# Transposing four normalised attention rows on TensorE instead of by DMA, with a new step list, in a gated SSM and linear-attention kernel

## The chip, the core and the metric

The kernel runs on one core of a Trainium2 chip. The time is device microseconds of one execution; lower is better. The profile is of one further execution. Engines: PE is TensorE (PEld its weight loads), DVE VectorE, ACT ScalarE, POOL GpSimd, SP the engine that issues most DMAs.

## The reference

The input x has 2048 rows of 512 (bf16). Two branches are computed from it and mixed, row by row, with a gate:

```python
g = sigmoid((x * gate_w).sum(-1, keepdims=True))
a = 2.0 * einsum("blp,dp->bld", h, C).real + x * Dskip   # h[t] = Lam_bar * h[t-1] + B_bar x[t], 512 complex states
q, k, v = split(x @ wqkv)                                # 32 heads of 16
phi(u) = concat(softmax(u @ w_phi), softmax(-(u @ w_phi)))
b = ((phi(q) @ (phi(k).T @ v)) / (phi(q) . sum(phi(k)) + 1e-6)) @ wo
out = g * a + (1 - g) * b
```

## The kernel before

The 2048 rows are taken as 16 tiles of 128; the rows of one tile share their index modulo 8 (`r`), so that the recurrence becomes eight interleaved ones of 256 steps. All tiles and weights stay in SBUF.

The program is written as small generators, one for each piece of work, and each `yield` ends a step. The string ORDER, a list of some 850 names, says in which order the steps are emitted; each engine then runs its own instructions strictly in that order, and waits on semaphores where data or a PSUM bank is not ready. In a name, `@5` gives the PSUM bank of the step, `:D` puts a copy out of PSUM on DVE instead of ACT, `:A` issues an output DMA from ACT instead of SP, and `F:36` emits 36 constant 128-column products on PE (L802) that keep PE busy and are not used.

The steps that matter here:

- `l8` to `l15`: SP loads one tile of x by a transposing DMA (L228); tiles 0 to 7 are loaded at the head of the program. `NR`, `NI`: SP loads the two halves of B into Bn (L283). `R0` to `R7`: SP transposes Bn into BT (L287). `Q`, `C`: SP transposes the query weights and C (L291, L295). `J`: SP moves C's parts into X1 and X2 (L300). `O`: SP loads Wo (L304).
- `W`, `f`: PE transposes the key weights C2r (L273) and folds w_phi into them (L430). `k`, `v`, `q`: PE projects a tile to keys, values or queries (L474, four 512-column matmuls), and ACT or DVE copies the bank out. `g<r><j>`: PE computes the inputs of the recurrence (L600 to L607, reading BT), and ACT copies to uv. `z`: the scan on DVE. `h<r><j>`: the states. `c`: two products by ACT from X1, X2 (L589) and a sum by DVE give the output matrix.
- `x`, `n`, `e`, `s` (and `X`, `N`, `E`, `S` for queries, in groups of four rows): maximum, minimum, exponential and normalisation of the features. The last steps of `S1` to `S3` issue four transposing DMAs each from SP, phT<-EEq (L562), the feature maps of four rows.
- `a`, `Y`: the sum over keys and its masked copy KVm.
- For each of the 16 output tiles n: `y` collects the SSM output in a PSUM bank (L716, two steps of four 512-column matmuls, then L721, four of 128); `o` has two halves of four 68-column matmuls pn (L735), from which ACT takes the logarithm of the denominator (ld) and ACT or DVE a copy (nu), then rd on ACT and the normalised row `on` on DVE (L743), then the transpose oT<-on by a DMA from SP (L748); `t` adds oT times Wo into the same bank (L755, four of 512), scales (L759, L761) and issues the output DMA (L763).

Two of these pieces, as they stand:

```python
oT = op_.tile([P, HG, P], BF16, name="oT", bufs=8)
live["oT", n] = oT
nc.sync.dma_start_transpose(out=oT[:], in_=on[:].rearrange("p g h e -> p (g h e)"))
```

Of the kernel before, what the change touches and what calls it, by code (L numbers as in the profile page):

```python
# [23 lines left out]
ORDER = """
NR B F:36 F:6 W0@0 W0:D NI W1@1 W2@2 W3@3 W1 f0@4 f0 W2:D W3:D f1@5 f2@6 f2:D f1 f3@0 f3 F:6 l9 V@1 V U U P k0@2 P P
V2@3 k0 P2 P2 U P2 V2 k1@4 k1 l10 P2 P2 P4 U P4 P3 P2 P3 k3@5 k2@7 P4 i0 i3 i0 i0 k2 i0 i3 v3@6 n0 v1@0 v0@1 x0 n0
k5@3 i3 i3:D i2 i0 l11 k6@2 l14 i3 x0 gw n0 i2 x0 k4@4 i1 v1 v6@7 k3 i2 i2:D x0 i1 l8 x0 i2 i1 i1:D i1 x1 n0 x1 n0 M
x1 n1 x1 n1 x1 n1 k5:D n1 L R0 k7@0 k7:D k6 k4 v3 n1 x2 R1 e0 e0 n2 l12 s0 n2 v5@5 v2@2 v2 e1 s0 n2 s0 v7@4 n2 v4@3 v4
k9@6 e1 k10@0 l15 x2 k11@2 s0 R5 l13 x2 s1 k8@3 x2 Q3 k10 s1 s0 s0 s0 v5 v6 v7 v0 k14@0 s1 g40@5 k14 D Q0 g00@7 g00 R3
s1 k8 a0@41 k12@0 a0 g40 x2 k12 n2 s1 s1 s1 k9 g20@7 g10@3 R2 g10 g20 Q1 g10 k11 x3 g50@5 n3 x3 n3 x3 n3 g30@0 g60@6  # L30
C0 e2 e2 x3 g60 a1 e2 a1 e2 k13@7 C5 g30 g30 n3 k15@3 k15 k13 x3 g21@2 n3 s2 s2 e3 C4 e3 x4 R4 s2 g01@6 g01 g50 g21
g50 x4 s2 g11@0 g41@3 s2 g51@7 s2 n4 g11 g70@6 x4 n4 g31@2 x4 n4 g11 s2 e3 e3 s3 Q2 g70 g70 g61@5 g70 z0 g41 z0 s3
w2@0 g31 g31 C6 n4 a2 C1 s3 g61 C2 C3 a2 a2 z0 C7 w3@6 a2 w3 g51 x4 g51 w2 n4 w0@3 w0 g02@2 z0 w1@5 w1 s3 g71@6 z0 g02
J2 g71 g71 g12@7 z0 g71 v8@0 J3 e4 e4 z1 v8 J2 g22@3 s3 g12 g22 z0 z0 g62@5 z1 z0 z0 q1@2 z1 s3 z1 z1 z1 R6 q0@6 J1
g12 J0 s3 q2@0 J3 e4 q0 z1 z1 e4 s4 g32@3 z1 z1 q3@7 q2 q1 q3 c2 s4 g32 g42@6 g42 xA g52@0 h10@2 h50@7 h50 R7 g43@6 J1
g62 g32 g52 c5 c5 J0 g52 g43 g03@5 nA xA c4 h60@3 c4 g72@7 h10 g72 g72 g72 h51@0 h11@6 v9@2 v9 h60 v11@3 c5 c1 xA nA
c1 h51 z2 s4 z2 g03 s4 v11 g23@0 g23 h61@7 z2 a3 O v10@2 v10 z2 z2 g63@5 g63 g13@3 g13 nA h11 nA a3 a3 c4 z2 a3 c0 g13
c1 z2 z2 xA z2 z2 h61 xA g33@6 g33 h12@0 c3 c3 c0 c0 s4 s4 g33 v14@2 v14 h12 g53@5 g53 g53 nA s4 h52@3 h52 eA g73@7
g73 h20@0 g73 g73 z3 z3 eA eA eA v12@6 v12 v15@2 v13@5 v13 q9@7 h20 z3 z3 c2 v15 h31@3 z3 z3 sA q8@0 h31 q8 z3 z3 a4
c2 q4@6 a4 a4 sA q4 h32@5 h32 z3 z3 a4 G q6@2 Y Y sA q9 h53@3 h53 sA c6 c6 sA h33@0 h41@6 h13@5 c3 q7@7 q7 h41 sA q6  # L40
h13 Y Y sA sA h03@4 sA h03 q13@3 h30@6 h30 sA q15@7 c6 h62@5 h33 h22@2 h22 q13 q15 h63@1 h62 q5@4 h63 h00@6 h23@0 h23
c7 c7 c7 sA h01@3 sA h43@2 h43 q5 h21@7 h02@5 h42@1 h42 h40@4 h01 h00 h40 y1@0 h21 h02 END X1 N1 y0@3 X1 N1 X1 o0@6 o0
o0@2 o0 q11@5 q11 o0 o1@1 o1 o1@4 o1 o1 G N1 q14@7 q14 X1 N1 X1 N1 q10@6 q10 X2 o3@2 o3 o3@5 N2 X2 N2 o1 o3 X2 o0 o0
o1 X2 y4@1 N2 X2 E1 E1 E1 E1 S1 o3 y1 y2@4 y4 y2 o2@7 o2 S1 o2@6 o2 y5@2 y5 q12@5 S1 S1 N2 o2 o2 o2 o3 o3 S1 y3@7 y3
S1 y3 N2 S1 q12 S1 S1 S1 S1 X3 G X3 N3 E2 E2 X3 G X3 E2 E2 y9@6 y9 y0 y0 t0 N3 X3 t0 t0 S2 S2 y2 y6@5 t2 S2 t2 t3 t3
y6 o4@3 o4 o4@4 o4 y5 o4 o4 y1 o5@7 o5 o5@3 o5 S2 y9 t1 S1 o5 S2 N3 N3 o5 t3 o6@4 o6 o6@7 y4 o4 y13@3 S2 o6 o5 N3 o6
o6 y8@4 y8 y13 o6 S2 t1 t4 S2 S2 S2 t4:D y6 t5 E3 E3 E3 E3 t5 S3 S3 o7@7 t4:A o7 o7@0 o7 o7 t6 y12@1 o8@2 o7 o8 o8@7
S3 o8 o8 S2 t6 S2 y12 S3 o7 S3 o8 o9@0 o9:D o9@2 o9 y11@7 o9 o8 S3 y7@5 o9 o9 S3 S3 o10@0 o10 y7 y10@2 S3 S3 S3 o11@0
o11 y7 t7 t7 y8 o11@0 o11 t8 t9 o10@5 t7:A y13 S3 o10 o10 y15@0 o10 t9 t8:D o12@5 o12:D y15 t2:A o12@6 o10 o11 o11 y10
y15 o11 o12 o12 o12 o14@4 o12 o14:D o14@5 o14 o14 o14 y10 y14@6 o13@4 o13 o13@5 o14 o13 o13 o13 t5:A y12 y11 o15@4  # L50
o15:D t9:A o15@5 o15:D o13 o15 o15 y14 y11 t11 o15 t10 t1:A y14 t11 t11:A t10 t10 t14 t14 t12 t12 t13 t6 t13:D t15
t8:A t14:A t13 t12:A t15 t15:A
"""
# [14 lines left out]
def kernel(  # L68
# [44 lines left out]
    def bank(shape, dtype, name):  # L113
        return ps.tile(shape, dtype, tag=f"t{sel['banks'].pop(0)}", name=name, bufs=1)

    def evac(out_ap, in_ap):
        if sel["eng"] == "act":
            nc.scalar.copy(out=out_ap, in_=in_ap)  # L118
        else:
            nc.vector.tensor_copy(out=out_ap, in_=in_ap)  # L120
# [15 lines left out]
    def aexp(**kw):  # L136
        ins = nc.scalar.activation(**kw)  # L137
# [586 lines left out]
    def st_o(n):  # L724
        ti = order[n]
        op_ = pools["op"][1]
        ph = phT0[:, n] if n < 4 else live["ph", n // 4][:, n % 4]
# [4 lines left out]
        for hf in range(2):
            pn = bank([P, 16, Dh + 1], F32, "pn")
            for m in range(4):
                MM(out=pn[:, 4 * m:4 * m + 4, :].rearrange("p h e -> p (h e)"), lhsT=ph[:, 4 * hf + m, :],  # L735
                   rhs=KVm[:, 4 * hf + m, :], start=(m == 0), stop=True, skip_group_check=True)
# [6 lines left out]
        VT(out=on[:].rearrange("p g h (a b) -> p (g h) a b", b=4), in0=nu[:].rearrange("p c h (a b) -> p (c h) a b", b=4),  # L743
           in1=rd[:].unsqueeze(2).to_broadcast([P, 32, Dh // 4, 4]), op=ALU.mult)
# [3 lines left out]
        nc.sync.dma_start_transpose(out=oT[:], in_=on[:].rearrange("p g h e -> p (g h e)"))  # L748
# [89 lines left out]
```

## Time and profile before

| | us |
|---|---|
| median of 3 runs (161.19 to 162.15) | 162.09 |
| the profiled execution | 161.69 |
| its span (first to last instruction) | 159.3 |
| PE busy | 148.9 |
| DVE busy | 130.7 |
| ACT busy | 129.3 |

Times within the profile count from the span's start. A row of a timeline gives the start, the length from the first to the last of a merged run, engine, line, operation, output <- input, shape and count; in brackets stands how long the engine was idle before it, and what ended that. A row of the groups gives line, engine, operation, names, forms and count, then the busy time and the mean of one in ns, then the idle time ahead and its causes. "To landing" is the time from a DMA's issue to its data being there. Matmuls overlap at their ends: a row of four with 512 columns lasts 1.03 us, and the next begins 0.86 after it.

### The profile page before, as it was taken

The page shows a single profiled execution, that of the slowest core. Times are in us where ns is not written, and L with a number is a line of the kernel's source. Part 1 is how long each engine was busy: PE and PEld are TensorE (multiplying, and loading weights), DVE is VectorE, ACT ScalarE, POOL GpSimd, SP SyncE. Part 2 cuts the span into 40 slices and gives each one's busy share as a digit, 9 for nine tenths or more (in the row PEclk, how much of TensorE's full clock was granted, in tenths as well). Part 3 has the DMA queues.
Part 4 walks back from the last instruction along what each step waited for, and adds up shares of the span by engine and source line. Part 5 has one row for each costly group of instructions (what it writes and reads, how often), then busy time and mean ns, then how long its engine had stood idle before and what let it go on. Part 6 is the DMA issues. An engine that isn't in the chain of part 4 may idle for free.

```text
span 159.3 us, 3368 instructions
## 1 busy us (share of the span) xinstructions
PE 148.9 (93%) x1250; PEld 96.1 (60%) x1250; DVE 130.7 (82%) x301; ACT 129.3 (81%) x277; POOL 16.4 (10%) x43
## 2 busy tenths in 40 slices
...
GB/s 124 149 205 121 214 165 94 113 84 99 103 97 99 107 187 204 230 7 0 0 0 4 0 0 168 101 0 66 45 123 184 123 170 185 87 210 171 196 188 110
DMA packets 53023, 18.06 MB, mean 113 GB/s; under 512 B 46352, under 2 KB 53008, under 8 KB 53008
## 3 DMA queue, kind: packets, MB, share of 16 engines
...
q0 software_dynamic: 160, 0.01, 0.2%
...
## 4 chain that ended last, share of the span: by engine, by line
SPq 35%; PE 24%; DMA 20%; DVE 9%; ACT 6%; issue 3%; DVEq 0%
SPq L228 14%; PE py L716 11%; SPq L287 8%; DMA oT<-on 7%; SPq L295 6%; PE py L755 5%; DMA phT<-EEq 5%; SPq L291 4%; PE pq L474 3%; DMA phT<-EEk 3%; SPq L300 3%; ACT EEk L137 3%; DMA X<-HM 2%; DVE Bn L671 2%; ACT va L118 2%
## 5 line engine op out<-in xcount | busy, mean ns | idle before, releaser
L600 PE MATMUL pgq<-xT,BT 128*128 128x256 bf16 x256 | 31.6, 273 | 1.2 <-ACT uv L118 1.2
L474 PEld LDWEIGHTS <-xT 128*128 128x128 bf16 x192 | 18.1, 97 | 18.1
L600 PEld LDWEIGHTS <-BT 128*128 128x128 bf16 x256 | 24.7, 98 | 6.0 <-issue 1.7
L137 ACT ACTIVATE EEk<-EEk 128x1024 bf16<-128x1024 bf16 x20 | 20.5, 1066 | 0.7 <-DVE EEk L526 0.6
L755 PE MATMUL py<-Wo,oT 128*128 128x512 bf16 x64 | 15.5, 379 | 1.3 <-DMA oT<-on 1.3
L118 ACT CAST uv<-pgq 128x512 bf16<-128x512 f32 x28 | 15.8, 595 | 0.6 <-PE pgq L607 0.4
L474 PE MATMUL pq<-Wq,xT 128*128 128x512 bf16 x64 | 15.9, 379 | 0.0
L474 PE MATMUL pk<-Wk,xT 128*128 128x512 bf16 x64 | 15.1, 379 | 0.0
L474 PE MATMUL pv<-Wv,xT 128*128 128x512 bf16 x64 | 15.1, 379 | 0.0
L743 DVE TENSOR_TENSOR on<-nu,rd 128x512 bf16<-128x512 bf16 x16 | 6.7, 422 | 10.3 <-ACT rd L137 8.1
L137 ACT ACTIVATE ld<-pn 128x16 f32<-128x16 f32 x32 | 6.0, 194 | 9.1 <-PE pn L735 8.9
L759 ACT ACTIVATE ot<-py,G 128x512 bf16<-128x512 f32 x13 | 9.0, 692 | 4.6 <-PE py L755 3.5
L137 ACT ACTIVATE EEq<-EEq 128x1024 bf16<-128x1024 bf16 x12 | 11.7, 1044 | 0.6 <-DVE EEq L526 0.6
L589 ACT ACTIVATE phT<-X,dgB 128x512 bf16<-128x512 bf16 x16 | 11.1, 746 | 1.2 <-DMA X<-HM 1.2
L735 PEld LDWEIGHTS <-phT 128*128 128x128 bf16 x128 | 6.0, 97 | 6.9 <-DMA phT<-EEq 3.0
L755 PEld LDWEIGHTS <-oT 128*128 128x128 bf16 x64 | 5.8, 98 | 7.2 <-DMA oT<-on 1.6
L118 ACT CAST nu<-pn 128x256 bf16<-128x256 f32 x27 | 9.9, 384 | 0.0
L547 DVE TENSOR_TENSOR EEk<-EEk,rck 128x4096 bf16<-128x4096 bf16 (+1 forms) x5 | 9.3, 1851 | 0.0
L118 ACT CAST vx<-pv 128x512 bf16<-128x512 f32 x16 | 9.1, 594 | 0.1
L118 ACT CAST Xq<-pq 128x512 bf16<-128x512 f32 x16 | 8.9, 608 | 0.1
L735 PE MATMUL pn<-KVm,phT 128*128 128x68 bf16 x128 | 7.2, 195 | 1.8 <-DMA phT<-EEq 1.2
L118 ACT CAST Xq<-pk 128x512 bf16<-128x512 f32 x14 | 8.1, 599 | 0.6 <-PE pk L474 0.5
...
## 6 DMA issues: line engine op xcount, KB each, us to landing
X<-HM SPq DMA_DIRECT2D x8, 256.0 KB, 4.1
out_dram<-ot ACTq DMA_DIRECT2D x11, 128.0 KB, 2.2
out_dram<-ot SPq DMA_DIRECT2D x5, 128.0 KB, 2.2
C2r<-in_B_wqkv_dram ACTq DMA_DIRECT2D x2, 256.0 KB, 3.5
...
```

What stands on the lines that cost most here:

```text
L118: nc.scalar.copy(out=out_ap, in_=in_ap)
L137: ins = nc.scalar.activation(**kw)
L228: nc.sync.dma_start_transpose(out=xT[:, :, ti * P:(ti + 1) * P], in_=x_res[ti // 2, ti % 2])
L287: nc.sync.dma_start_transpose(out=BT[:, :, t, :], in_=Bn[:, t, :])
L295: nc.sync.dma_start_transpose(out=CA[:, ri, kt, :], in_=(A_C_re, A_C_im)[ri][:, kt * P:(kt + 1) * P])
L474: MM(out=pt[:], lhsT=xT[:, kt, ti * P:(ti + 1) * P], rhs=W[:, kt, :], start=(kt == 0), stop=(kt == KT - 1))
L547: VT(out=E5, in0=E5, in1=rc.to_broadcast([P, L, 2 * NB, Dh, 4]), op=ALU.mult)
L589: nc.scalar.mul(out=t_, in_=x_, mul=c_)
L600: MM(out=pg[:, h, :], lhsT=BT[:, kt, 2 * j + h, :], rhs=xT[:, kt, r * NC:(r + 1) * NC], start=(h == 0 and kt == 0), stop=(r % 2 == 0 and k ...
L716: MM(out=py[:], lhsT=hs(r, t, slice(a * P, (a + 1) * P)), rhs=C2B[t], start=(t == 0), stop=False)
L735: MM(out=pn[:, 4 * m:4 * m + 4, :].rearrange("p h e -> p (h e)"), lhsT=ph[:, 4 * hf + m, :], rhs=KVm[:, 4 * hf + m, :], start=(m == 0), st ...
L755: MM(out=py[:], lhsT=oT[:, g, :], rhs=Wo[:, g, :], start=False, stop=(g == HG - 1))
```

## The change

For rows 12 to 15 the transpose of `on` is made by four 128x128 PE transposes into a bank, and the bank is copied to oT, on DVE for rows 12, 13 and 14 and on ACT for row 15. The other rows keep the DMA. The constant products fall from 48 (42 in one stretch, then 6) to 36 (32, then 4). The step list is written anew: the steps are the same, with one more for each of the four rows, in another order and with other banks and engines. All line numbers behind the imports move by one, and those behind the `o` step by ten.

```diff
 ORDER = """
-NR B F:36 F:6 W0@0 W0:D NI W1@1 W2@2 W3@3 W1 f0@4 f0 W2:D W3:D f1@5 f2@6 f2:D f1 f3@0 f3 F:6 l9 V@1 V U U P k0@2 P P
+B F:28 l11 F:4 W1@0 W0@1 W2@2 W1:D f1@3 W3@4 f1 W0:D f0@5 f0 NR W2:D f2@6 W3:D f3@0 f3 f2:D V@1 V P P P P2 P2 P2 P2 P2
...
-o15:D t9:A o15@5 o15:D o13 o15 o15 y14 y11 t11 o15 t10 t1:A y14 t11 t11:A t10 t10 t14 t14 t12 t12 t13 t6 t13:D t15
-t8:A t14:A t13 t12:A t15 t15:A
+y10 o15 o15@5 o15:D o15 o13 t12 o15 o14@7 o14 o14 t12:D t12 t11 t11:D o15@5 o15 o13@7 t10 t6:A t11 y15 o13:D t10 t10
+t15 t15 t15:A o14 o14@2 t13 o14:D t13 t13 t14 t14 t14:A
 """
 H_VECTOR = tuple((r, j) for r in (1, 2, 4, 5, 6) for j in range(4))
+OT_PE = (12, 13, 14, 15)
...
         oT = op_.tile([P, HG, P], BF16, name="oT", bufs=8)
         live["oT", n] = oT
-        nc.sync.dma_start_transpose(out=oT[:], in_=on[:].rearrange("p g h e -> p (g h e)"))
+        on2 = on[:].rearrange("p g h e -> p g (h e)")
+        if n in OT_PE:
+            po = bank([P, HG, P], BF16, "po")
+            for g in range(HG):
+                nc.tensor.transpose(po[:, g, :], on2[:, g, :], ident[:])
+            yield
+            evac(oT[:], po[:])
+            yield
+            return
+        nc.sync.dma_start_transpose(out=oT[:], in_=on2.rearrange("p g f -> p (g f)"))
         yield
```

Four places where the list moves instructions. On SP, the loads at the head of the program, before:

```order
L237 DMA Wv<-in_B_wqkv_dram 128x4x512
L228 DMA_TRANSPOSE xT<-in_A_x_dram 128x4x128 x4
L283 DMA Bn<-in_A_B_re_dram 64x8x512
L283 DMA Bn<-in_A_B_im_dram 64x8x512
L228 DMA_TRANSPOSE xT<-in_A_x_dram 128x4x128 x5
L287 DMA_TRANSPOSE BT<-Bn 128x4x128 x2
L228 DMA_TRANSPOSE xT<-in_A_x_dram 128x4x128 x2
```

and after:

```order
L238 DMA Wv<-in_B_wqkv_dram 128x4x512
L229 DMA_TRANSPOSE xT<-in_A_x_dram 128x4x128 x5
L284 DMA Bn<-in_A_B_re_dram 64x8x512
L229 DMA_TRANSPOSE xT<-in_A_x_dram 128x4x128
L284 DMA Bn<-in_A_B_im_dram 64x8x512
L229 DMA_TRANSPOSE xT<-in_A_x_dram 128x4x128 x5
L288 DMA_TRANSPOSE BT<-Bn 128x4x128 x4
```

Tiles 11 and 12 of x now stand among the loads of Bn, and the first BT transposes behind 15 tiles of x instead of 13 (four tiles stand ahead of Wv in both). Tile 13 is the last of the 15, and PE reads it in k13, two tiles ahead of the first `g`; ahead of that first `g` stand 23 tiles of k and v instead of 21.

On ACT, around the first products that read X (phT is the space of their results), before:

```order
L137 ACTIVATE EEk<-EEk 128x1024
L118 CAST Xq<-pq 128x512 x3
L589 ACTIVATE phT_116<-X_138,dgB 128x512
L118 CAST uv_132<-pgq 128x512 x3
L589 ACTIVATE phT_116<-X_138,dgB 128x512
L589 ACTIVATE phT_116<-X_139,dgB 128x512
```

and after:

```order
L119 CAST Xq<-pq 128x512 x2
L138 ACTIVATE EEk<-EEk 128x1024
L119 CAST uv_132<-pgq 128x512 x2
L119 CAST vx_91<-pv 128x32x16
L590 ACTIVATE phT_116<-X_138,dgB 128x512
L119 CAST uv_132<-pgq 128x512
L590 ACTIVATE phT_116<-X_139,dgB 128x512
```

Counted from the start of ACT's list, three copies to uv and two to vx more now stand ahead of the first such product.

On SP, the end of the program, before:

```order
L562 DMA_TRANSPOSE phT<-EEq 128x8x128 x3
L763 DMA out_dram<-ot 128x512
L562 DMA_TRANSPOSE phT<-EEq 128x8x128
L763 DMA out_dram<-ot 128x512
L748 DMA_TRANSPOSE oT<-on 128x4x128 x3
L562 DMA_TRANSPOSE phT<-EEq 128x8x128 x4
L748 DMA_TRANSPOSE oT<-on 128x4x128 x3
L562 DMA_TRANSPOSE phT<-EEq 128x8x128 x4
L748 DMA_TRANSPOSE oT<-on 128x4x128 x6
L763 DMA out_dram<-ot 128x512 x3
```

and after:

```order
L563 DMA_TRANSPOSE phT<-EEq 128x8x128 x4
L758 DMA_TRANSPOSE oT<-on 128x4x128 x3
L563 DMA_TRANSPOSE phT<-EEq 128x8x128 x4
L758 DMA_TRANSPOSE oT<-on 128x4x128 x3
L563 DMA_TRANSPOSE phT<-EEq 128x8x128 x4
L758 DMA_TRANSPOSE oT<-on 128x4x128
L773 DMA out_dram<-ot 128x512
L758 DMA_TRANSPOSE oT<-on 128x4x128
L773 DMA out_dram<-ot 128x512 x4
```

Behind the last four feature maps stand two transposes of rows instead of six, and no output DMA stands between the maps of groups 1 and 2 and the rows any more. The load of Wo, which stood behind the X transfers, now stands behind the first four maps (phT_116).

On PE, the steps from row 12's first half to the end (a and b are the halves of pn, T the new transpose; y and t are four matmuls of 512 columns, yD four of 128), read off the two lists:

```
before  12a y15 12b y10 y15D 14a 14b y10D y14 13a 13b y12D y11 15a 15b y14 y11D t11 t10 y14D t14 t12 t13 t15
after   12a 12b y15 13a 13b y14 y14D T12 14a y10 15a y10D 15b t12 14b t11 T15 T13 t10 y15D t15 T14 t13 t14
```

Two steps of 512 columns and two of 128 stand ahead of row 12's first half that stood behind it, and the four T are new.

More of the change, by code (lines that the diff above doesn't have):

```diff
@@ L24 @@
 ORDER = """
-NR B F:36 F:6 W0@0 W0:D NI W1@1 W2@2 W3@3 W1 f0@4 f0 W2:D W3:D f1@5 f2@6 f2:D f1 f3@0 f3 F:6 l9 V@1 V U U P k0@2 P P
[L26 to L49, printed above, removed]
@@ L50 @@
-y15 o11 o12 o12 o12 o14@4 o12 o14:D o14@5 o14 o14 o14 y10 y14@6 o13@4 o13 o13@5 o14 o13 o13 o13 t5:A y12 y11 o15@4
-o15:D t9:A o15@5 o15:D o13 o15 o15 y14 y11 t11 o15 t10 t1:A y14 t11 t11:A t10 t10 t14 t14 t12 t12 t13 t6 t13:D t15
-t8:A t14:A t13 t12:A t15 t15:A
+B F:28 l11 F:4 W1@0 W0@1 W2@2 W1:D f1@3 W3@4 f1 W0:D f0@5 f0 NR W2:D f2@6 W3:D f3@0 f3 f2:D V@1 V P P P P2 P2 P2 P2 P2
+P4 U P3 P4 P4 i1 i2 U l12 i1 i2 U F:4 k0@2 k0 NI P2 P3 l10 i0 l9 k1@3 k1 x0 i1 i1 i0 i2 k3@4 l14 x0 k2@5 n0 U M i1 k2
@@ new lines @@
+V2@6 v3@1 i2 x0 i0 v0@7 i0:D i0 v2@0 x0 k3 l8 n0 l13 i3 x0 k5@2 k5 i3 k4@3 v0 R0 x1 k6@5 n0 n0 i3 i3:D x1 x1 i2 k4 n0
+v1@4 i3 L V2 k7@2 k7 n1 n1 x1 n1 gw x1 n1 R1 v6@7 e0 e0 v1 k6:D v4@6 n1 x2 n2 v7@3 v7 k11@2 v6 s0 x2 s0 e1 n2 s0 v5@5
+v5 s0 s0 R2 D k12@4 R3 k10@3 k9@7 v4 k8@5 n2 l15 s0 e1 k13@6 v2 s1 k10 k14@0 s0 k11 C1 Q2 k8 C4 g20@3 s1 x2 k13 a0@25
+k14 a0 n2 s1 k12 g20 x2 g00@6 k9 g30@0 s1 s1 s1 x2 n2 s1 v3 g40@4 x3 g01@3 g10@7 n3 R5 g00 a1 a1 x3 g60@1 n3 e2 R4
+g11@6 g10 x3 g01 n3 e2 x3 e2 e2 n3 g11 k15@3 g60 g10 g30 g40 x3 s2 n3 g70@1 k15 g11 s2 x4 s2 s2 n4 g30 Q1 Q3 x4 n4 e3
@@ new lines @@
+e3 x4 C5 n4 Q0 x4 g50@7 g50 g50 s2 g21@4 n4 g21 s2 s2 v8@3 e3 e3 s3 g70 g70 g70 z0 s3 z0 g31@6 g31 s3 z0 z0 v11@0
+g41@7 a2 C6 a2 g41 z0 z0 v11 g61@4 a2 g61 C7 w0@1 w0 C3 w1@7 w1 g31 a2 w2@0 w2 w3@4 s3 s3 g51@1 g51 g51 z0 R7 z0 x4
+g62@7 w3 z0 z0 g71@6 g71 g02@0 v8 n4 s3 J2 g71 g71 z1 g02 z1 h50@1 h50 J2 z1 e4 e4 q1@4 h10@3 g62 g12@6 h10 g22@0 q2@1
+z1 z1 z1 g22 q2 s3 z1 z1 q1 e4 h60@3 h60 g12 g12 z1 q3@7 q0@0 q0 q3 g32@1 e4 xA C2 g42@4 g32 nA g32 s4 g42 v9@6 v9 z1
+s4 C0 J0 J0 g52@0 g52 c4 g52 nA c4 xA c4 R6 g72@7 g72 J1 s4 nA g23@3 g43@1 g03@4 g63@6 g72 g72 z2 h51@0 J3 c5 a3 g23
```

14 lines of the change are left out of this document (added).

## The prediction

> **What bounds the kernel now.** I read the page first, then the stretches, then the waits of the two ends. The page's first line:
>
> ```profile
> PE 148.9 (93%) x1250; PEld 96.1 (60%) x1250; DVE 130.7 (82%) x301; ACT 129.3 (81%) x277; POOL 16.4 (10%) x43
> ```
>
> PE is the engine with the least slack, so its gaps are the first thing to price. From the view by stretches (columns: stretch, length, busy time and instructions of PE, PEld, DVE, ACT, POOL, granted clock, DMA share, GB/s):
>
> ```profile
> 15.00:20.00 5.00, 5.00 (x25) 2.23 (x23) 5.00 (x19) 4.97 (x11) 4.61 (x11) 1.00 1.19 211
> 60.00:70.00 10.00, 9.10 (x76) 7.12 (x74) 8.52 (x20) 8.77 (x18) 0.00 (x0) 1.00 0.74 168
> 80.00:90.00 10.00, 9.17 (x93) 5.53 (x91) 9.90 (x21) 9.81 (x18) 0.00 (x0) 1.00 0.01 2
> 100.00:110.00 10.00, 9.34 (x71) 4.64 (x70) 10.00 (x22) 9.28 (x28) 0.00 (x0) 1.00 0.27 53
> 130.00:135.00 5.00, 4.57 (x38) 2.13 (x37) 3.94 (x10) 3.69 (x16) 0.00 (x0) 1.00 1.03 203
> 135.00:140.00 5.00, 4.23 (x34) 2.25 (x32) 0.66 (x1) 1.77 (x7) 0.00 (x0) 1.00 0.86 100
> 140.00:145.00 5.00, 4.37 (x36) 2.17 (x34) 2.36 (x5) 2.65 (x9) 0.00 (x0) 1.00 1.09 185
> ```
>
> In the middle PE, DVE and ACT are all nearly full, and one dent stands out, 60 to 70. From 130 on DVE and ACT are half empty, PE has gaps of 0.4 to 0.8 in each 5 us, and the DMA engines are full. What holds the end is therefore SP's queue and the transfers it issues. SP's own timeline of the tail (start, length, line, what, how many):
>
> ```profile
> 127.35 5.83 SPq L562 DMA_TRANSPOSE phT<-EEq  x4
> 133.28 4.42 SPq L748 DMA_TRANSPOSE oT<-on  x3
> 137.80 5.69 SPq L562 DMA_TRANSPOSE phT<-EEq  x4
> 143.58 8.39 SPq L748 DMA_TRANSPOSE oT<-on  x6
> ```
>
> SP is busy without a break from 127.35 to 151.97: 17 transposes at 1.4 us each. PE's side of it, and DVE's last big product:
>
> ```profile
> 134.43 1.23 DVE L558 TENSOR_TENSOR EEq<-EEq,rhoq 128x2048 bf16<-128x2048 bf16 x1
> 142.21 0.30 PE L735 MATMUL pn<-KVm,phT 128*128 128x68 bf16 x4 [0.22 <-DMA phT<-EEq]
> 145.09 0.43 PE L735 MATMUL pn<-KVm,phT 128*128 128x68 bf16 x8 [0.51 <-DMA phT<-EEq]
> 151.74 3.63 PE L755 MATMUL py<-Wo,oT 128*128 128x512 bf16 x16 [0.50 <-DMA oT<-on]
> ```
>
> The product that frees group 3's maps ends at 135.66; SP, still at oT, issues their transposes from 137.80; the first lands for PE at 142.21. From there to PE's end (151.74 + 3.63 = 155.37) pass 13.16 us, then 3.93 to the span's end (the last product, its output DMA).
>
> **The change, part by part. The tail.** Four of the last six oT transposes leave SP: 4 x 1.4 = 5.6 us of its queue, all in the stretch that nothing hides. In their place PE gets 16 matmuls of 128 columns and the four copies go one to ACT and three to DVE. Prices of PE, from the chain, and of the copies, from the groups:
>
> ```profile
> 116.27 0.86 PE py L755 x4
> 117.13 0.22 PE py L721 x4
> 120.81 0.26 PE pn L735 x8
> L118 ACT COPY Xq<-ptw 128x512 bf16<-128x512 bf16 x1 | 0.6, 587 | 3.5 <-PE ptw L273 3.5
> L120 DVE COPY Xq<-ptw 128x512 bf16<-128x512 bf16 x3 | 1.2, 421 | 1.8 <-PE ptw L273 1.8
> ```
>
> So PE gets 4 x 0.22 = 0.9 us more work, DVE 1.3, ACT 0.6; DVE and ACT have room (2.36 and 2.65 of 5 us busy), so theirs costs nothing unless a wait is queued on it. Now PE's work from the first pn of row 12 to its end, counted from the step lists. Before: 11 groups of four 512-column matmuls, 5 of four 128-column, 8 pn halves: 9.5 + 1.1 + 1.0 = 11.6 us, and 13.16 passed, so 1.6 of waits. After: 9, 7 and 8: 7.7 + 1.5 + 1.0 = 10.2 us. Two steps of y with 512 columns and two with 128 went ahead of the maps. The maps are spaced by 5.69 / 4 = 1.42, so row 15's lands 4.27 after row 12's; the work listed ahead of its pn is 3.7, a wait of 0.6. That makes 10.8, plus 0.2 for the last matmul's drain: 11.0. I add 0.35 for the new hand-over (pn, ld, rd, on, transpose, copy) in one place or another and take 11.35, a gain of **1.8 us**. The bounds: 2.1 (no hand-over shows) and nothing (rival B).
>
> Is a DMA transpose dear at all? The page's list of issues (KB each, us to landing), and one output's issue in SP's timeline:
>
> ```profile
> out_dram<-ot SPq DMA_DIRECT2D x5, 128.0 KB, 2.2
> oT<-on SPq DMA_TRANSPOSE x16, 2.6
> phT<-EEq SPq DMA_TRANSPOSE x12, 4.0
> 122.99 0.35 SPq L763 DMA_DIRECT2D out_dram<-ot  x1
> ```
>
> To landing, an oT transpose takes hardly longer than a plain output. [...]
>
> **The start.** The first stretch of constant products falls from 42 to 32, the second from 6 to 4.
>
> ```profile
> 1.11 4.66 PE L802 MATMUL spin<-fillw 128*128 128x128 bf16 x42 [1.11 <-DVE fillw L156]
> 0.79 1.07 ACTq L164 DMA_DIRECT2D C2r<-in_B_wqkv_dram  x2
> C2r<-in_B_wqkv_dram ACTq DMA_DIRECT2D x2, 256.0 KB, 3.5
> 6.00:6.50 0.50, 0.50 (x7) 0.50 (x6) 0.26 (x1) 0.00 (x0) 0.00 (x0) 1.00 0.91 58
> 7.00:7.50 0.50, 0.50 (x12) 0.42 (x9) 0.50 (x2) 0.31 (x2) 0.00 (x0) 1.00 0.94 159
> ```
>
> The 42 run at 0.105 each and end near 5.5; 32 end near 4.5. The weights that W needs land at 0.79 + 3.5 = 4.3 and about 4.8, and the second half is wanted only eight transposes later: nothing waits. But PE runs at half pace until about 6.7 (7 matmuls in half a us, then 12), whatever it runs, so ten dropped matmuls are worth ten at the later pace, 10 x 0.055 = 0.55, and the two others 0.1. **Gain 0.7** on PE; bounds 0 and 1.2.
>
> **SP's first loads.** x tiles 11 and 12 move up among the loads of Bn, and the first two BT transposes go behind 15 tiles of x instead of 13.
>
> ```profile
> 22.32 2.50 SPq L287 DMA_TRANSPOSE BT<-Bn  x2
> 26.93 1.91 PE L600 MATMUL pgq<-xT,BT 128*128 128x256 bf16 x16
> BT<-Bn SPq DMA_TRANSPOSE x8, 2.5
> DMA to landing us min/median/max: 2.8/4.5/7.0
> ```
>
> (The last row is that of tile xT's 16 loads.) Two more at 1.26 put the BT issues at 24.9 and 26.1, landing at 28.7. The first g now stands behind two more k/v tiles: 26.93 + 1.7 - 0.7 = 27.9, its second half at 28.4: a wait of 0.3. Tile 13, the last of the 15, is issued at 23.6 and wanted by k13 at 26.2; with the fastest landing it comes at 26.4, with the median at 28.1. PE showed no wait in this stretch before. I take **0.6 lost**; bounds 0 and 4.3 (rival C).
>
> **The middle.** The dent at 60 to 70:
>
> ```profile
> 61.98 0.72 ACT L589 ACTIVATE phT<-X,dgB 128x512 bf16<-128x512 bf16 x1 [0.67 <-DMA X<-HM]
> 63.23 1.07 PE L600 MATMUL pgq<-xT,BT 128*128 128x256 bf16 x8 [0.90 <-ACT uv L118]
> 65.28 0.72 ACT L589 ACTIVATE phT<-X,dgB 128x512 bf16<-128x512 bf16 x1 [0.51 <-DMA X<-HM]
> ```
>
> ACT stands 1.2 us for the X transfers, three uv evictions queue behind it, and PE waits 0.9 for a bank. In the new list three uv and two vx evictions more stand ahead of the first product that reads X, over 2 us of ACT's work, so the transfers should be there. I take back **0.9**, PE's wait; bounds 0 and 1.5 (DVE's idle time in that stretch). The load of Wo moves from SP's idle time after the X transfers to behind the first four phT; SP waits there too, for the first attention row, and Wo is read by the t steps alone, which come later still: nothing; its issue would cost SP about 1 us if that idle time were gone, as much as one transpose.
>
> Group 3's maps thus come 0.7 - 0.6 + 0.9 = **1.0 us earlier**. PE must by then have done more (the steps of y, 1.7 + 0.4, less the fills, 0.7: 1.4 us); it has gaps of 0.9 + 0.8 + 0.7 + 0.4 + 0.8 + 0.6 = 4.2 in the stretches shown, so there is room for both. SP allows it: the product was 2.1 us ahead of its issue, and the two output DMAs that stood between transposes on SP (one is the row at 122.99) are gone.
>
> **Sum.** 159.3 - 1.8 - 1.0 = 156.5 of span. The profiled execution took 161.69, 2.39 outside its span: 158.9. The median shown is 162.09, 0.4 above the profiled run: **159.3 us**.
>
> **The rivals. A, more gain.** If SP's queue closes up and ACT and DVE pass on all they save, the maps come up to 3.0 earlier (SP's 2.1 plus the 0.9 of the middle), and the tail gains its full 2.1: 162.1 - 5.1 = 157.0. For it: SP's unbroken queue. Against: ACT and DVE are nearly full in the middle, and PE's own gaps would nearly all have to vanish. 0.12.
>
> **B, the waits move into PE's queue: no change.** The transposes stand in PE's line ahead of products that were free to run. A row's way from pn to transpose is pn, ld, rd, on, and each of these stands behind others on ACT and DVE:
>
> ```profile
> L137 ACT ACTIVATE rd<-ld,nge 128x128 bf16<-128x128 f32 x16 | 6.9, 428 | 0.2 <-issue 0.2
> L743 DVE TENSOR_TENSOR on<-nu,rd 128x512 bf16<-128x512 bf16 x16 | 6.7, 422 | 10.3 <-ACT rd L137 8.1
> L137 ACT ACTIVATE ld<-pn 128x16 f32<-128x16 f32 x32 | 6.0, 194 | 9.1 <-PE pn L735 8.9
> ```
>
> That is about 0.3 + 0.2 + 0.4 + 0.4 = 1.3 alone, 0.9 more if another row's go first; row 12's transpose has 2.2 us of work between, row 15's 1.9. Half a us lost at each of the four costs 2 us and the tail's 1.8 is gone: 162.1 - 1.0 = 161.1. [...] 0.24.
>
> **C, the early loads come late: slower.** In 15 to 20 the DMA engines are overfull (share 1.19), and the slowest tile took 7.0. If tile 13 takes that, it lands at 30.6, PE stands 4.3 us from 26.2, and k9 to k14 feed the whole chain of features on DVE, which has no slack to win it back; the start's head start is spent, and the tail's gain remains: 162.1 - 1.8 + 4.3 = 164.6. It decides once the landing takes over 4.4 (2.6 of margin plus the tail's 1.8). Against it: the tiles with 6 and 7 us stood right behind Bn's 1 MB, and tile 13 is now seven issues behind it. 0.14.
>
> **How the numbers follow.** Forecast 0.50, A 0.12, B 0.24, C 0.14. A measurement of this kernel tells about 1% (1.6 us) from no change. The forecast and A are faster by more than that: 0.62. B, and the mildest of C, lie within: 0.25. The rest of C: 0.13. The forecast's own range is 158.3 to 160.4; the range goes down to just under A, 156.8, and up through B and half of C to 162.8.
>
> **What would show it.** Right: the first W near 4.5; SP's last oT issued before 147 and only two behind the last maps; first pn of row 12 near 141; 11 to 11.5 us from there to PE's end; no wait on X in the middle. Wrong: a wait of PE at k8 to k13 or the first g above 1 us (C); gaps ahead of the po transposes adding to 2 us (B); first maps at 142 or later, which would mean that ACT or DVE, not SP, set them.

## The result, and the profile after

| | before | changed |
|---|---|---|
| median, same chip | 162.12 us (4 runs, 161.19 to 162.42) | 156.52 us (4 runs, 156.21 to 157.09) |
| ratio | | 0.967 (95%: 0.962 to 0.972) |
| the profiled execution / its span | 161.69 / 159.3 | 156.63 / 154.6 |

The change makes the kernel 5.6 us faster, twice the 2.8 of the forecast, and the time lies below the low end of the range. Ratios, here and below, compare undisturbed executions alone; of the first two runs that mend the old list, that leaves three and five of ten.

The page of the changed kernel, the engines' busy time and the chain that ended last, and under them the chain of before:

```profile
PE 147.7 (96%) x1254; PEld 95.6 (62%) x1254; DVE 131.8 (85%) x303; ACT 129.4 (84%) x279; POOL 16.1 (10%) x43
DVE 47%; PE 32%; DMA 8%; ACT 6%; issue 4%; DVEq 0%; SPq 0%
SPq 35%; PE 24%; DMA 20%; DVE 9%; ACT 6%; issue 3%; DVEq 0%
```

SP's queue, 35% of the chain before, is no longer in it: nearly half of the span goes back to DVE. The stretches that the prediction showed (length, then busy time of PE, PEld, DVE, ACT, POOL, clock, DMA):

```profile
60.00:70.00 10.00, 10.00 (x95) 8.22 (x93) 9.88 (x25) 9.81 (x19) 0.00 (x0) 1.00 0.61 113
80.00:90.00 10.00, 10.00 (x98) 6.18 (x97) 9.91 (x26) 9.83 (x18) 0.00 (x0) 1.00 0.01 2
100.00:110.00 10.00, 9.88 (x69) 5.00 (x68) 9.97 (x23) 8.78 (x25) 0.00 (x0) 1.00 0.32 83
130.00:135.00 5.00, 5.00 (x47) 2.94 (x46) 2.28 (x4) 2.69 (x11) 0.00 (x0) 1.00 0.87 175
135.00:140.00 5.00, 4.42 (x41) 2.42 (x38) 1.08 (x2) 2.63 (x10) 0.00 (x0) 1.00 0.87 140
140.00:145.00 5.00, 5.00 (x55) 2.98 (x52) 2.37 (x7) 3.16 (x14) 0.00 (x0) 1.00 1.15 244
```

The dent at 60 to 70 is gone on all three engines (PE 9.10 to 10.00, DVE 8.52 to 9.88), and so are PE's gaps at 80 to 90 and most of those at 100 to 110. SP's timeline, first maps of the keys and then the tail:

```profile
92.58 6.55 SPq L563 DMA_TRANSPOSE phT<-EEk  x4
...
124.40 5.40 SPq L563 DMA_TRANSPOSE phT<-EEq  x4
129.89 4.30 SPq L758 DMA_TRANSPOSE oT<-on  x3
134.30 6.69 SPq L563 DMA_TRANSPOSE phT<-EEq  x4
141.08 1.25 SPq L758 DMA_TRANSPOSE oT<-on  x1
142.38 0.57 SPq L773 DMA_DIRECT2D out_dram<-ot  x1
143.04 1.22 SPq L758 DMA_TRANSPOSE oT<-on  x1
```

Group 3's maps are issued at 134.30 instead of 137.80, and SP's last transpose is over at 144.26 instead of 151.97. DVE's product that frees these maps (L559) runs from 132.37 for 1.22, so it ends at 133.59 instead of 135.66. So of the 3.5 us by which the maps are issued earlier, 2.1 come from the product and 1.4 from SP, which stood 2.1 behind it and now stands 0.7. PE's tail:

```profile
137.07 1.04 PE L765 MATMUL py<-Wo,oT 128*128 128x512 bf16 x4 [0.57 <-DMA oT<-on]
...
139.80 0.42 PE L736 MATMUL pn<-KVm,phT 128*128 128x68 bf16 x8
...
142.38 0.39 PE L753 MATMUL po<-ident,on 128*128 128x128 bf16 x4
...
146.01 0.61 PE L753 MATMUL po<-ident,on 128*128 128x128 bf16 x8
146.93 1.04 PE L765 MATMUL py<-Wo,oT 128*128 128x512 bf16 x4 [0.31 <-DMA oT<-on]
...
148.89 0.39 PE L753 MATMUL po<-ident,on 128*128 128x128 bf16 x4
149.11 1.89 PE L765 MATMUL py<-Wo,oT 128*128 128x512 bf16 x8
```

No bracket stands at the first pn of row 12 (139.80) nor at any of the four transposes po: PE arrives there without waiting. Group 3's maps took 3.3 to 4.7 us to land, so the first was there by 139.0: it is PE's own work, and no longer SP's transfers, that sets when row 12 begins. From 139.80 to PE's end (149.11 + 1.89 = 151.00) pass 11.2 us, then 3.6 to the span's end.

So the span's 4.7 us are: the first pn of row 12 comes 2.4 earlier (142.21 to 139.80), the tail is 1.96 shorter (13.16 to 11.2), what follows PE's end 0.33 (3.93 to 3.6). The forecast had 1.0 and 1.8. The question for the experiments was where the other 1.4 came from.

### The profile page after: what moved, and what is told of

Same layout as the page of the kernel before. It is cut to its first block, busy times and chain, and to the rows that moved or that the text cites. A ratio compares the mean times of both kernels' runs of the same rounds, so it can differ in the third digit from the quotient of the medians.

```text
span 154.6 us, 3382 instructions
## 1 busy us (share of the span) xinstructions
PE 147.7 (96%) x1254; PEld 95.6 (62%) x1254; DVE 131.8 (85%) x303; ACT 129.4 (84%) x279; POOL 16.1 (10%) x43
## 4 chain that ended last, share of the span: by engine, by line
DVE 47%; PE 32%; DMA 8%; ACT 6%; issue 4%; DVEq 0%; SPq 0%
PE py L717 9%; DVE smk L511 6%; PE pk L475 6%; DMA oT<-on 5%; PE py L765 5%; PE pgq L601 4%; DMA phT<-EEq 3%; DVE Bn L672 3%; DVE EEk L548 3%; DVE w L641 3%; DVE HM L672 3%; DVE H L652 3%; PE spin L812 3%; DVE EEk L527 2%; DVE EEk L521 2%
## 5 line engine op out<-in xcount | busy, mean ns | idle before, releaser
L765 PE MATMUL py<-Wo,oT 128*128 128x512 bf16 x64 | 16.1, 379 | 0.9 <-DMA oT<-on 0.9
L119 ACT CAST uv<-pgq 128x512 bf16<-128x512 f32 x28 | 16.3, 604 | 0.3
L475 PE MATMUL pv<-Wv,xT 128*128 128x512 bf16 x64 | 15.6, 379 | 0.0
L769 ACT ACTIVATE ot<-py,G 128x512 bf16<-128x512 f32 x12 | 8.0, 684 | 3.5 <-PE py L765 3.3
L736 PEld LDWEIGHTS <-phT 128*128 128x128 bf16 x128 | 6.7, 98 | 5.3 <-DMA phT<-EEq 1.2
L736 PE MATMUL pn<-KVm,phT 128*128 128x68 bf16 x128 | 8.0, 194 | 0.8 <-DMA phT<-EEq 0.7
L511 DVE TENSOR_TENSOR smk<-smk 128x512 bf16<-128x512 bf16 (+4 forms) x18 | 8.6, 476 | 0.1
```

The costliest lines, as they stand in the source:

```text
L475: MM(out=pt[:], lhsT=xT[:, kt, ti * P:(ti + 1) * P], rhs=W[:, kt, :], start=(kt == 0), stop=(kt == KT - 1))
L511: VT(out=dst, in0=cur[:, :, :, 0:n, :], in1=cur[:, :, :, n:2 * n, :], op=op)
L765: MM(out=py[:], lhsT=oT[:, g, :], rhs=Wo[:, g, :], start=False, stop=(g == HG - 1))
L769: nc.scalar.mul(out=ot[:], in_=py[:], mul=G[:, ti:ti + 1])
```

## Where the lead arises: DVE's account

The view by stretches, cut at 20, 60 and 90 us, and SP's first maps. Before:

```profile
0.00:20.00 20.00, 18.89 (x134) 12.31 (x135) 14.97 (x68) 13.54 (x28) 11.97 (x31) 1.00 0.89 163
20.00:60.00 40.00, 39.82 (x380) 29.74 (x379) 39.84 (x77) 39.42 (x71) 4.48 (x13) 1.00 0.64 115
60.00:90.00 30.00, 27.93 (x281) 20.51 (x279) 28.32 (x63) 27.64 (x53) 0.00 (x0) 1.00 0.25 57
```

```profile
94.98 6.65 SPq L562 DMA_TRANSPOSE phT<-EEk  x4
```

Changed:

```profile
0.00:20.00 20.00, 18.74 (x128) 11.36 (x129) 16.09 (x71) 14.48 (x29) 13.44 (x39) 1.00 0.71 152
20.00:60.00 40.00, 39.69 (x380) 29.64 (x379) 39.81 (x76) 39.22 (x73) 2.63 (x5) 1.00 0.68 122
60.00:90.00 30.00, 30.00 (x298) 22.32 (x296) 29.67 (x67) 29.46 (x55) 0.00 (x0) 1.00 0.21 38
```

The third busy time of a row is DVE's. It did 1.12 us more by 20, 0.03 less from 20 to 60, 1.35 more from 60 to 90: 2.44 in all, and the first maps leave 94.98 - 92.58 = 2.40 earlier. PE's busy time gives no such account (88.43 by 90 against 86.64, a difference of 1.8, and it has 12 constant products fewer in it). Over the runs below this holds throughout: DVE's busy time by 90 us and the time of the first maps add up to the same 178.0 to 178.8 us, while each of them moves by over 5.

Two things limit this account. ACT's closes nearly as well: its busy time by 90 and the first maps add up to 175.0 to 176.2 over the same kernels, PE's to 180.2 to 183.5. So the sums set DVE and ACT apart from PE; that it is DVE rather than ACT rests on the chain alone (DVE 47%, ACT 6%). And one pair of executions does not give the lead of the start: the kernels with the old list's start have 14.97 to 16.16 of DVE by 20, those with the new one's 36 products 15.65 to 16.21. The gain from 60 to 90 is clear of such scatter: 27.87 to 28.32 in the five kernels that have the old list up to there and load C by transposing DMAs (one with fewer constant products), 29.67 in all five that have the new list with its own loads.

| kernel | DVE busy to 90 | first maps issued | sum | group 3's maps to the span's end | row 12's first pn to PE's end |
|---|---|---|---|---|---|
| before | 83.1 | 94.98 | 178.1 | 21.5 | 13.2 |
| changed | 85.6 | 92.58 | 178.2 | 20.3 | 11.2 |
| 48 products in the new list | 84.4 | 93.72 | 178.1 | 19.1 | 10.6 |
| 36 products in the old list | 83.1 | 95.64 | 178.7 | 21.9 | 14.2 |
| the same, two c and the last BT moved | 82.4 | 96.29 | 178.7 | 21.7 | 14.0 |
| old list, PE rows | 82.1 | 96.50 | 178.6 | 21.8 | 14.4 |
| new list, DMA end | 85.7 | 92.42 | 178.1 | 21.8 | 12.2 |
| old list, plain C | 85.1 | 92.96 | 178.0 | 21.9 | 14.2 |
| new list, plain C | 85.2 | 93.08 | 178.3 | 20.4 | 10.6 |
| new work, old loads | 80.1 | 98.58 | 178.7 | 19.9 | 10.9 |
| old work, new loads | 79.8 | 98.98 | 178.8 | 22.8 | 15.0 |
| old list, new end with PE | 83.0 | 95.33 | 178.3 | 19.4 | 10.6 |
| old list, new end with DMA | 83.2 | 95.23 | 178.4 | 23.2 | 14.5 |
| old list, new end with PE, plain C | 85.3 | 93.12 | 178.4 | 19.1 | 10.6 |

The last two columns show the tail. From group 3's maps to the span's end it takes 19.1 to 20.4 wherever the four rows go through PE in the new order of the end, 21.5 to 23.2 elsewhere in the table (the first run below, with 27.7, is a case of its own). From row 12's first pn to PE's end it is 10.6 to 11.2 with that end, whatever the middle, and 13.2 to 15.0 with the old one (12.2 and 14.5 with the end made for DMAs). Here 1.4 of the difference is work that the new list puts ahead of row 12 (11.6 us of listed work against 10.2); the rest is waits. In four of the six kernels with the new end this stretch is 10.64, and no wait of PE shows in it.

## The experiments

**The four rows by DMA again, in the new list.**

```diff
-OT_PE = (12, 13, 14, 15)
+OT_PE = ()
```

and the copy step that each of the four rows then lacks is taken out of the list.

> The changed kernel with rows 12 to 15 transposed by DMA again, at the same places of the new step list (nothing else differs). Theory T (the transposes carry the tail): the last row's transpose is issued where its PE transpose stood, near 148.9, behind an output DMA, and takes 2.6 us to land instead of about 0.8 for PE and copy, and the four issues of 1.4 us come one behind another with the outputs: PE ends 2 to 3 us later, the time is 158.5 to 159.5. Rival L (the new list carries the tail, the transposes are hidden by the steps of y and t between): PE ends at most 0.6 us later, 156.5 to 157.1.

Measured: 163.91 us, 1.012 (1.007 to 1.018) of before; 7.4 over the changed kernel. PE in this run:

```profile
144.62 0.29 PE L736 MATMUL pn<-KVm,phT 128*128 128x68 bf16 x4
148.00 1.04 PE L765 MATMUL py<-Wo,oT 128*128 128x512 bf16 x4 [3.09 <-DMA oT<-on]
148.87 0.29 PE L736 MATMUL pn<-KVm,phT 128*128 128x68 bf16 x4
```

The direction was foreseen, the size not: t12 stands early in the list, PE stands 3.09 us before it, and a pn of row 14 stands behind it; further waits of 1.67, 0.26 and 2.00 follow. The list's end fits PE transposes and nothing else, so this loss is no measure of what the transposes bring.

**The constant products alone.** The new list with 42 and 6 (`F:28` to `F:38`, the last `F:4` to `F:6`), and the old list with 32 and 4 (`F:36` to `F:26`, the last `F:6` to `F:4`).

> The changed kernel with the constant products of before, 42 and 6. Theory T (nothing in the new list swallows a lead on the way, so the start counts in full): PE's first useful work moves from 4.5 back to 5.6, DVE's feature work starts 1 us later, and the end moves by the 0.7 to 1.0 that PE's pace there gives: 157.2 to 157.6. Rival (the lead is swallowed by PE's wait for tile loads near 25 and by the other engines): 156.3 to 156.8.

> The kernel before with the constant products of the change, 32 and 4, and nothing else. Theory S (SP's chain of loads, unbroken from 0.8 to 65, sets when X and the last BT are there, and ACT, PE and DVE meet that chain at 62 to 66): the lead of the start is lost there, 161.8 to 162.3, no change. Rival (the start adds up with everything else): 161.0 to 161.5.

Measured: 156.87 us in the new list, 0.35 over the changed kernel and within the scatter (0.966 of before on its own chip, where the changed kernel has 0.967); 162.34 in the old, 1.000 (0.996 to 1.003). The old list with fewer products, in stretches:

```profile
0.00:20.00 20.00, 18.67 (x129) 10.90 (x130) 16.72 (x72) 15.42 (x30) 13.68 (x38) 1.00 0.79 164
20.00:60.00 40.00, 38.35 (x371) 28.82 (x370) 38.23 (x73) 37.73 (x68) 2.81 (x6) 1.00 0.68 114
60.00:90.00 30.00, 27.55 (x280) 20.39 (x278) 28.10 (x61) 27.25 (x52) 0.00 (x0) 1.00 0.30 59
```

DVE is 1.75 ahead of before by 20 (16.72 against 14.97) and has lost 1.61 of it by 60 and 0.22 more by 90. In the old list something in the middle takes a start's lead away.

**PE rows in the old list.** The four rows go through PE; in the old list only the end is edited so that their eighth step and their banks fit.

> The kernel before with only the new transposes: rows 12 to 15 by PE, copied out by DVE, in the old step list, each T put one or two steps further back so that it finds a free bank. Theory L (in the old list PE still has 11.6 us of steps behind row 12's first map, and gets 0.9 more): of the 1.6 us of waits about 1 goes, the end moves by -0.5 to +0.2 us, 161.6 to 162.3. Rival T (taking four transposes off SP is the gain by itself): 160.0 to 160.6.

Measured: 161.97 us, 1.000 (0.996 to 1.004), as theory L had it. The group 3 stretch is 21.8, no shorter than before. This kernel has before's instructions up to the tail, yet its first maps leave at 96.50 instead of 94.98: in the old list the middle differs by 1.5 us from one execution to another, and the execution from which the prediction was made was an early one. The new list differs too, by 1.0 (92.42 to 93.42 in three kernels that are the same up to there). So the pair's lead of 2.40 is one value of a range, and even the nearest two executions, 94.98 and 93.42, are 1.6 apart.

**Mending the old list at the place that the prediction saw.** The first two products from X moved behind the evictions that they delayed; then the last BT transpose put earlier on SP; then fewer constant products as well.

```diff
-... q3@7 q2 q1 q3 c2 s4 g32 ... g52 c5 c5 J0 g52 ... c4 g72@7
+... q3@7 q2 q1 q3 s4 g32 ... g52 J0 g52 ... c4 c5 c5 c2 g72@7
-... R6 q0@6 J1 ... h50 R7 g43@6
+... R6 R7 q0@6 J1 ... h50 g43@6
```

> The kernel before; the first products of c2 and c5, the ACT products that waited for the X transfers at 61.98 and 65.28, are moved behind those of c4. Theory S (the meeting of ACT with SP's chain at 62 to 66 is the dent, and it delays all that follows): ACT's waits for X go, DVE's idle time in 60 to 70 falls from 1.5 to under 0.7, the maps of group 3 come about 1 us earlier, 160.9 to 161.6. Rival (the last BT, landing at 63.7, holds PE there anyway): 161.9 to 162.4.

> As the one before, and R7, the last BT transpose, is issued right behind R6 instead of behind three of the X transfers. Theory S: both things that ACT and PE met at 62 to 66 are out of the way, PE is full from 60 to 70, the maps of group 3 come 1.4 to 2 us earlier, 160.2 to 161.0. Rival (the middle gives nothing by itself, whatever it saves is lost to the waits of the end): 161.8 to 162.4.

> As the one before, with 32 and 4 constant products. Theory S: with the dent gone the start's lead is no longer lost there and adds 0.4 to 1.0 to the run before, 159.6 to 160.4. Rival (the start gives nothing in any list, as 48 of them in the new list cost only 0.35): the same as the run before within 0.4.

Measured: ratios 1.001 (0.992 to 1.009), 1.004 (0.996 to 1.011), 1.009 (1.005 to 1.013). No gain, the third a little slower. Its waits (us in total, times, the longest) still have ACT's for X, and one of DVE behind it:

```profile
ACT phT L589 <- DMA X<-HM: 1.0, 1, 1.0
DVE C2i L593 <- ACT phT L589: 1.8, 1, 1.8
```

ACT's wait stands at 66.95 instead of 61.98 and 65.28, where it was 1.2 in all, and DVE's busy time from 60 to 90 is 27.64 against 28.32. Moving these steps moved the wait.

**The new list without PE transposes, with an end made for DMAs.** Up to row 12 the changed kernel's list, then the remaining steps in an order in which each `t` stands later.

> The changed kernel up to row 12's first map; rows 12 to 15 by DMA again, and the steps behind it in an order that suits that: all pn first, SP's six row transposes together, the products and outputs behind. Theory M (the PE transposes are worth about the time that SP needs for the last issues): the sixth row transpose is issued near 148 and lands near 150.7, PE ends near 151.8, 157.2 to 157.9. Rival T (with DMA the new list cannot hold its gain, as in the run with only the transposes undone): 160 or more.

Measured: 158.74 us, 0.980 (0.972 to 0.988). The first maps leave at 92.42 and group 3's at 134.17, as in the changed kernel. The time lies between the two expected ranges. So the new order up to row 12 is worth about 2.0% without any PE transpose, and the transposes with their end bring the other 1.3% (0.980 to 0.967).

**Is it SP's chain of loads?** C is loaded by plain DMAs, in the old list and in the new. This leaves out the transposition of C; shapes and all later steps stay.

```diff
-        nc.sync.dma_start_transpose(out=CA[:, ri, kt, :], in_=(A_C_re, A_C_im)[ri][:, kt * P:(kt + 1) * P])
+        nc.sync.dma_start(out=CA[:, ri, kt, :], in_=(A_C_re, A_C_im)[ri][kt * P:(kt + 1) * P, :])
```

> The kernel before, with the eight loads of C made by plain DMAs instead of transposing ones (this leaves out the transposition of C; every shape and every later step stays). SP's unbroken chain of loads before 65 us gets shorter by about 8 x 0.7 = 5.6 us; nothing else changes. Theory S (in the old list SP's loads, not the engines, hold the middle back): the waits on X, on the query weights' and C's space and on the last BT go, 159.5 to 161.0 us. The rival (the gain of the new list is the order of the work on PE, ACT and DVE; SP's chain is only a bystander): 161.7 to 162.6, no change.

> The changed kernel, with the same edit: C loaded by plain DMAs, its transposition left out. Theory S: the new list reads every load later than it lands, so a shorter chain is worth under 0.4 us, 156.1 to 156.9. If SP's loads still hold the new list in the middle, it gains 1 us or more: 155.5 or less.

Measured: 160.31 us in the old list, 0.987 (0.980 to 0.994), as the theory had it; 157.22 in the new, 0.7 over the changed kernel's first measurement with overlapping runs (156.00 to 158.07; 0.966 of before on its own chip, against 0.967), a little outside the expected band and in any case no gain. SP's first transfers of X before, then with plain C in the old list, and the stretches of the latter:

```profile
52.46 2.15 SPq L300 DMA_DIRECT2D X<-HM  x3
...
47.16 2.15 SPq L300 DMA_DIRECT2D X<-HM  x3
...
92.96 5.33 SPq L562 DMA_TRANSPOSE phT<-EEk  x4
```

```profile
20.00:60.00 40.00, 40.00 (x383) 29.78 (x382) 39.84 (x77) 39.37 (x71) 3.93 (x10) 1.00 0.78 138
60.00:90.00 30.00, 29.17 (x289) 21.48 (x288) 29.74 (x67) 28.53 (x55) 0.00 (x0) 1.00 0.14 30
```

X goes out at 47.16 instead of 52.46, DVE's dent from 60 on is gone (29.74, where the changed kernel has 29.67), and the first maps leave 2.0 earlier. The order of the work is the old one: what held the old middle back was the arrival of SP's loads. The new list is past that; a shorter chain gives it nothing.

**Order of loads or order of work?** All load steps are taken out of one list and put ahead of everything else in the order of the other, so that SP follows the one and the engines the other.

```diff
-B F:28 l11 F:4 W1@0 ... NR W2:D ... l12 ...
+B NR NI l9 l10 l11 l14 l8 R0 R1 l12 l15 R5 l13 ... F:28 F:4 W1@0 ... W2:D ...
```

> The changed kernel with the load steps (x tiles 8 to 15, Bn, BT, query weights, C, X, Wo) taken out of its list and put ahead of everything else in the order of the list before, so that SP issues them in the old order and PE, ACT and DVE do their work in the new one. Theory S as it stands (the new list reads every load later than it lands, in whatever order): 156.3 to 157.5. Theory U (order of loads and order of use belong together): waits of PE on x tiles 13, 14 or BT early on, 158.5 or more.

> The kernel before with its load steps put ahead of everything else in the order of the changed kernel's list: new order on SP, old work on PE, ACT and DVE. If the order of SP's loads carries the gain of the middle: 159.0 to 160.0. Theory U: the old work meets loads that now come later (the first BT behind 15 tiles of x, C's parts and X), 163 or more. Theory S with the order of the work as the carrier: 162 to 163, no gain.

Measured: 162.76 us (new work, old loads), 1.004 (1.000 to 1.008) of before; 166.02 (old work, new loads), 1.021 (1.014 to 1.029). Each is slower than the kernel that it was made from, by 6.2 and 3.7. PE and the clock in the first:

```profile
23.10 1.80 PE L475 MATMUL pk<-Wk,xT 128*128 128x512 bf16 x4 [2.00 <-DMA xT<-in_A_x_dram]
24.68 1.92 PE L475 MATMUL pv<-Wv,xT 128*128 128x512 bf16 x4
27.49 3.63 PE L475 MATMUL pk<-Wk,xT 128*128 128x512 bf16 x16 [0.89 <-DMA xT<-in_A_x_dram]
```

```profile
22.00:24.00 2.00, 0.90 (x3) 0.42 (x4) 1.97 (x6) 1.96 (x4) 1.06 (x2) 0.81 1.23 240
24.00:26.00 2.00, 2.00 (x7) 0.61 (x4) 1.97 (x5) 0.00 (x0) 0.00 (x0) 0.50 0.34 66
```

PE waits 2.00 for a tile of x, then runs at half the clock, then waits again. SP did follow the other list's loads: its first transfers of X leave at 52.91 and 49.68, against 52.46 and 48.87 in the lists that they were taken from. So neither half of the new list gains by itself. That fits a gain from each load standing where its reader comes later than it lands; which loads and readers matter, the two runs do not tell.

**The tail by itself.** The old list's first 549 steps (to the last products of the states), then the changed kernel's list from there, with PE transposes; the same with the DMA end; the first with plain C besides, its transposition left out.

> The list before up to the last products of the states (549 steps), then the changed kernel's list from there on, with its PE transposes of rows 12 to 15. Old start and middle, new end. Theory T1 (the tail's gain of 1.96 us stands by itself, in its own order of steps): 159.8 to 160.8. The rival T2 (the tail gains only where the middle has given it a lead; in the old list nothing, as with the transposes put into the old tail): 161.7 to 162.6.

> The same cut, but the end with all rows transposed by DMA, in the order that was made for that (as in the run of the new list with a DMA tail). Old start and middle, DMA end. T1 and T2 both: 161.5 to 163.0, about the kernel before; it is the base line of the run above. If it is under 161, the new order from the queries' features on carries part of the gain by itself.

> The run with the old start and middle and the new end with PE transposes, and C loaded by plain DMAs besides (its transposition left out). If the middle's share (2.0 us by SP's shorter chain) and the tail's add: 157.6 to 158.8. If the one takes the place of the other: 159.5 or more.

Measured: 161.94 us, 0.995 (0.992 to 0.999); 166.01, 1.021 (1.014 to 1.028); 160.19, 0.986 (0.978 to 0.993). By the times alone the first falls to the rival T2. But the second, which was to be the base line near 162, shows that the seam itself costs: the two lists do the queries in different orders, and at the cut PE waits,

```profile
100.82 1.02 PE L475 MATMUL pq<-Wq,xT 128*128 128x512 bf16 x4 [1.18 <-DVE Bn L672]
```

DVE stands 2.6 us for ACT's copies of the queries, and group 1's maps leave at 118.69 instead of 115.57. Against its own base line the PE end is worth 4.1 us, of which a part is the DMA end's waits for oT (4.7 us of PE in the whole run, 1.8 in the run with PE). The stretch behind the seam is free of it; SP's rows for group 3's maps, with PE and with DMA:

```profile
140.36 5.41 SPq L563 DMA_TRANSPOSE phT<-EEq  x4
```

```profile
140.77 5.73 SPq L563 DMA_TRANSPOSE phT<-EEq  x4
```

To the ends of the spans, 159.8 and 164.0, they leave 19.4 and 23.2, where before has 21.5. The new end is thus about 2 us shorter than the old one on an old middle too, and from row 12's first pn to PE's end it is the same 10.64 there as on a new middle. That is read from stretches: in the time of the whole kernel the seam hides it. And plain C takes 1.75 us off the run with the PE end (161.94 to 160.19), nearly the 2.0 that it took off before, so middle and tail seem to add; the 160.19 itself lies in the range that was expected if they did not, and only the seam's cost speaks against that reading.

## Why the prediction was wrong, point by point

**Tail: right in size, by partly other waits.** 1.8 forecast, 1.96 measured; 11.35 us from row 12's first pn to PE's end, measured 11.2. SP's last oT stands before 147 and two behind the last maps, as said, and rival B's waits ahead of the four transposes don't exist. But neither of the forecast's two waits is there. The 0.6 for row 15's map isn't, since the maps land before PE comes; the 0.35 for hand-overs isn't, since the one wait, the 0.31 at 146.93, is that of t10, whose row still goes by DMA. Four other kernels with this end need 10.64 and show no wait. That 11.35 came so close is luck in this part, and so is the 1.96: it is counted from an execution with a short old end, 13.16, where the other kernels of the table that keep it have 14.0 to 15.0. That the end needs its own order is shown by the runs of the old list with PE rows (no gain) and of the new list with DMA rows (7.4 lost).

**The maps' lead: wrong, and this is the step that failed.** "Group 3's maps thus come 0.7 - 0.6 + 0.9 = 1.0 us earlier" measured 2.4 (by the first pn of row 12; the maps themselves are issued 3.5 earlier, and PE, which waited for them before, now comes after they have landed). The three terms were priced on PE, in its busy time and waits; DVE's busy time, or ACT's, accounts for the first maps, and PE's does not. The middle was sized too small, and the loss at the first loads was not there. By DVE's rows:

- *Start*, forecast +0.7: +1.12 of DVE by 20. PE's rows:

```profile
1.11 3.59 PE L812 MATMUL spin<-fillw 128*128 128x128 bf16 x32 [1.11 <-DVE fillw L157]
4.50 1.08 PE L274 MATMUL ptw<-ident,C2r 128*128 128x128 bf16 x12
...
7.46 3.62 PE L475 MATMUL pk<-Wk,xT 128*128 128x512 bf16 x16
```

  The first W stands near 4.5 as forecast, and the first k at 7.46, against 8.57 before: 1.1 earlier. In this pair the dropped products gave their 0.105 each, not the 0.055 of the later pace at which they were priced. But "half pace until about 6.7, whatever it runs" does not hold from one execution to the next: in the changed run the pace rises near 5.1 already (7 matmuls from 4.50 to 5.00, 10 in the next half us, 12 from 6.00 to 6.50), and with the same 48 products the first k comes at 7.37 to 8.57 in the kernels with the old list, and at 7.34 to 8.09 in those with the new list and 36. So the 1.1 is in part the pair's, and the 0.7 is neither confirmed nor refuted. The run with 48 in the new list is only 0.35 slower: not all of such a lead reaches the end.
- *First loads*, forecast -0.6: the first g comes at 28.02, close to the 27.9 forecast, and PE shows one wait, of 0.31:

```profile
23.69 4.49 PE L475 MATMUL pk<-Wk,xT 128*128 128x512 bf16 x20 [0.31 <-ACT EEk L138]
```

  At the same place two other kernels with this list wait 0.20 and 0.53 for a tile of x. DVE lost 0.03 from 20 to 60. A delay of PE was counted that DVE hardly saw; that it had features of earlier tiles to work on is argued.
- *Middle*, forecast +0.9: +1.35 of DVE from 60 to 90 (1.35 to 1.80 over the kernels above), the term that is wrong clear of scatter. I took PE's wait for a bank and named DVE's idle time there, 1.5, as the upper bound; DVE's was the price. The cause was seen at the right place, the X transfers, but too narrowly: only the waits around the first products from X were priced, and the runs with those products moved gained nothing, while a shorter chain of loads gained 2.0. From 60 to 110 PE's gaps shrink from 2.73 to 0.12. I had counted them as room for work, not as time to win.

**Rival A** (157.0) came nearest to what happened: ACT and DVE pass on what they save, and SP closes up, by 1.4 of its 2.1. It got 0.12, because PE's own gaps "would nearly all have to vanish". They did: of the 4.2 us in the six stretches counted there, 0.7 are left. **Rival C's** late tile 13 is read by the fourth of the five tiles in the row at 23.69, behind the wait and with none of its own.

**The rest of the miss.** 156.5 of span were forecast and 154.6 measured: 1.4 by the lead, 0.15 by the tail, 0.33 behind PE's end. Outside the span 2.03 us instead of 2.39, and a median 0.1 below the profiled execution where 0.4 above was assumed, make 0.4 and 0.5 more: 2.8 in all.

**What stays open.** In the old list, shorter loads are shown to buy 2.0; that it is the same 2 us which the new order wins is argued, from the dent that vanishes in both and from plain C giving the new list nothing. How much the fewer constant products give at the start, and how much of it reaches the end (0.35 in the one comparison of times, within the scatter), is not settled, nor which single step of the list matters most.
